# Delta-rule attention and a gated feed-forward on one Trainium2 core: the attention's fp16 pairs and block matrices become fp32 products of one head each

## The chip, the cores and the metric

The kernel runs on one NeuronCore of a Trainium2 chip. The time is device microseconds from one launch; the time before is the median of three runs. The engines that matter are TensorE (PE in the profile, with its weight loads listed as PEld), VectorE (DVE), ScalarE (ACT), GpSimd (POOL) and SyncE (SP), which issues the DMAs.

## The reference

Two parts follow each other. The first is a recurrence over 768 tokens for 4 x 8 = 32 independent heads with 48 features each; the second is a dense product with a gate.

```python
# q, k, v: (4, 8, 768, 48); beta: (4, 8, 768)
k_n = k / (norm(k) + 1e-6)
for t in range(768):
    y[t]   = q[t] @ state                       # state: 48 x 48 per head
    v_old  = state^T k_n[t]
    state += beta[t] * outer(k_n[t], v[t] - v_old)
x = y, heads side by side                       # (3072 tokens, 384)
out = ((x @ w_a) * (x @ w_b)) @ w_out           # w_a, w_b: 384 x 1536, w_out: 1536 x 384
```

## The kernel before

**Chunks.** The recurrence is done in 24 chunks of 32 tokens, in six groups of four (`GROUPS`). The 128 partitions hold four heads' worth of 32 tokens (index `h4`), and eight such fours (index `q`) lie beside each other. The state of all heads lives in PSUM (`S_ps`, 112 partitions by 2 x 384). For every chunk there are: the Gram matrix `ga` of keys with keys and queries (`prep`); a triangular system whose inverse is built row by row on VectorE, with two instructions per row (`solve`, buffers `b`, `tmp`); and in `steps` the products `ks` (keys with state), `up` (inverse with right-hand side), `yp` (queries with state, plus masked attention with `u`) and the update of `S_ps`.

**Precision.** The products of the attention are fp16 with each operand split in a high and a low half, so each product is three matmuls (`THREE`: hi.hi, hi.lo, lo.hi). The halves are made by a ScalarE copy and a subtraction on VectorE, or through TensorE (`VIA_PE`: a matmul by the identity `eye`, a matmul by the negative identity `neg` or `neg1`, a copy out of PSUM). Keys are scaled by 1/norm; queries and values are scaled by a power of two that is found from sums of squares for each group (`total`, `gram`, `qtok` and `vn` loads in `prep`), and `facs` undoes it at the end.

**Block matrices.** `kqbd` (112 x 2 x 16 x 128, four of them) and `tabd` (128 x 2 x 2 x 8 x 128, two of them) hold the heads' small matrices on block diagonals with zeros between them, so that one 112 x 64 or 128 x 128 matmul serves two or four heads. GpSimd and VectorE zero them at the start; VectorE and ScalarE copy the blocks in for every chunk (`kqbd<-kqc`, `tabd<-ta`). The key norms reach the feature-major layout through a DRAM scratch tensor (`rk`, then `rbk`), for group 0 through a matmul.

**Feed-forward.** The weights come as 64-bit floats and are decoded by integer instructions on VectorE in four parts of columns (`weights`, streams `w0`, `w0b`, `w1`, `w2`), then split in halves. `moe` takes two chunks at a time (256 tokens, `xsub`) and walks 12 column blocks `fc`: 18 matmuls of 128 x 128 by 256 (`bank<-x,wsl`), the gate (`a`, `g`, `ghl`), and 6 matmuls by 384 columns (`bank<-wo_hi,ghl`, `bank<-wo_lo,ghl`). There are 12 x 12 = 144 such units.

**Order.** Nothing is issued in program order. `Plan` collects the operations, gives each a modelled duration (`price`) and a priority (`URGENCY` by stream), finds dependencies by the regions that are read and written, and list-schedules all engines in several passes; each engine then gets its instructions in that order. Six PSUM banks are leased to attention, gate and output in turn. Since one helper (line 402) records every instruction, nearly all have the same line in the profile; tiles tell them apart.

**Halved solves.** For groups where `HALVES` is 1 the system of 32 rows is solved as two of 16 in the same instructions (15 rows of steps in place of 31), and the corner is filled with small fp32 matmuls (`bank<-b,ta`, `bank<-b,mk`, `bank<-wr,b`).

## Time and profile before

| | |
|---|---|
| Time, median of three runs (lowest to highest) | 701.37 us (699.37 to 702.09) |
| Span of the profiled execution | 698.7 us |
| PE busy / PEld busy | 644.0 us / 546.2 us |
| DVE busy / ACT busy / POOL busy | 553.3 us / 334.6 us / 27.5 us |
| Mean granted TensorE clock | 0.957 |
| Matmul records | 11454 |
| DMA | 58.36 MB in 32863 packets |

The profiled execution is one of the same program; its span, 698.7 us, lies 2.7 us under the runs' median, and no more of its own time than the span is listed. Busy times are the union of an engine's instructions. A matmul's listed duration includes the time until its result is out (about 0.18 us for the smallest), so that several overlap; what a group costs on the PE is read from its start to the start of the next group in the order of time.

### The profile page before, as it was taken

The page shows a single profiled execution, that of the slowest core. Times are in us where ns is not written, and L with a number is a line of the kernel's source. Part 1 is how long each engine was busy: PE and PEld are TensorE (multiplying, and loading weights), DVE is VectorE, ACT ScalarE, POOL GpSimd, SP SyncE. Part 2 cuts the span into 40 slices and gives each one's busy share as a digit, 9 for nine tenths or more (in the row PEclk, how much of TensorE's full clock was granted, in tenths as well). Part 3 has the DMA queues.
Part 4 walks back from the last instruction along what each step waited for, and adds up shares of the span by engine and source line. Part 5 has one row for each costly group of instructions (what it writes and reads, how often), then busy time and mean ns, then how long its engine had stood idle before and what let it go on. Part 6 is the DMA issues. An engine that isn't in the chain of part 4 may idle for free.

```text
span 698.7 us, 25936 instructions
## 1 busy us (share of the span) xinstructions
PE 644.0 (92%) x11454; PEld 546.2 (78%) x11454; DVE 553.3 (79%) x1385; ACT 334.6 (48%) x786; POOL 27.5 (4%) x50
## 2 busy tenths in 40 slices
PE   2774999899989999999999998999899999999996
PEld 0443668788868888888888887888788888888886
DVE  8999889899657889998899997799797899643221
ACT  2374867655434446455545544445354334342222
POOL 9300000000000000000000000000000000000000
PEclk9976899999968999999999999999999999999999
DMA  9637756314212413243223232132231000100000
GB/s 228 179 111 215 220 151 195 101 35 136 71 60 69 111 40 100 63 106 92 71 69 96 56 100 81 46 92 76 72 88 49 2 22 27 37 26 1 12 13 23
DMA packets 32863, 58.36 MB, mean 84 GB/s; under 512 B 5104, under 2 KB 23280, under 8 KB 32752
## 3 DMA queue, kind: packets, MB, share of 16 engines
q1 hardware_dynamic: 32752, 56.72, 28.6%
q8 instruction: 89, 1.46, 0.9%
q14 instruction: 22, 0.18, 0.1%
HBM read 51.90 MB, written 4.80 MB: 81 GB/s over the span
## 4 chain that ended last, share of the span: by engine, by line
PE 81%; DVE 9%; DMA 5%; issue 3%; ACT 1%; SPq 0%; DVEq 0%; ACTq 0%
PE bank L402 78%; PE S_ps L402 3%; DMA wsl<-in_kqt 2%; DMA raw<-in_kqt 1%; DVE kqc L402 1%; DVE b L402 1%; DVE kqbd L402 1%; DVE wsl L402 1%; DVE tabd L402 1%; DVE x L402 1%; DMA b<-in_wa 1%; DMA t<-in_vn 1%; DVE raw L402 0%; DVE tmp L402 0%; DVE ghl L402 0%
## 5 line engine op out<-in xcount | busy, mean ns | idle before, releaser
L402 PE MATMUL bank<-x,wsl 128*128 128x256 f16 x2592 | 314.0, 275 | 1.7 <-issue 1.1
L402 PEld LDWEIGHTS <-wsl 128*128 128x128 f16 (+1 forms) x2676 | 249.4, 99 | 68.7 <-issue 22.7
L402 PE MATMUL bank<-wo_hi,ghl 128*128 128x384 f32 x576 | 187.4, 364 | 0.3 <-issue 0.2
L402 ACT COPY a<-bank 128x256 f32<-128x256 f32 x144 | 53.6, 372 | 141.3 <-PE bank L402 141.0
L402 PEld LDWEIGHTS bank<-wo_hi,ghl 128*128 128x128 f32 x576 | 107.9, 190 | 3.2 <-issue 0.6
L402 DVE TENSOR_TENSOR g<-bank,a 128x256 f32<-128x256 f32 x144 | 60.7, 421 | 59.8 <-ACT a L402 56.5
L402 PE MATMUL bank<-wo_lo,ghl 128*128 128x384 f32 x288 | 97.9, 340 | 0.0
L402 ACT CAST ghl<-g 128x256 fp32r<-128x256 f32 x144 | 58.1, 404 | 54.7 <-DVE g L402 54.0
L402 PEld LDWEIGHTS <-kqbd 112*64 112x64 f16 x3360 | 60.3, 115 | 17.7 <-issue 13.1
L402 DVE TENSOR_TENSOR ghl<-g,ghl 128x256 fp32r<-128x256 f32 x144 | 60.2, 419 | 14.9 <-ACT ghl L402 14.3
L402 PEld LDWEIGHTS bank<-wo_lo,ghl 128*128 128x128 f32 x288 | 55.2, 192 | 0.3 <-issue 0.2
L402 DVE TENSOR_TENSOR b<-b,tmp 128x31 f32<-128x31 f32 (+20 forms) x154 | 49.3, 320 | 2.1
L402 DVE TENSOR_TENSOR tmp<-b,b 128x31 f32<-128x31 f32 (+20 forms) x154 | 49.0, 318 | 2.1
L402 PE MATMUL bank<-shl,kqbd 112*64 112x48 f16 x2208 | 44.7, 192 | 0.6 <-issue 0.6
L402 DVE COPY tabd<-ta 32x1024 f16<-32x1024 f16 (+1 forms) x96 | 38.6, 402 | 5.4 <-PE bank L402 2.2
L402 PEld LDWEIGHTS <-tabd 128*128 128x128 f16 x1152 | 34.2, 97 | 5.4 <-issue 2.9
L402 ACT ACTIVATE ld<-ld 128x384 f32<-128x384 f32 x60 | 31.2, 522 | 12.9 <-DMA ld<-in_kn 11.0
L402 DVE COPY kqbd<-kqc 48x2048 f16<-48x2048 f16 x48 | 33.6, 701 | 3.1 <-PE bank L402 2.5
L402 PE MATMUL S_ps<-uhl,khl 32*48 32x48 f16 x2208 | 23.5, 186 | 8.8 <-issue 8.7
L402 PEld LDWEIGHTS <-khl 32*48 32x48 f16 x2208 | 20.3, 97 | 13.6 <-issue 12.7
L402 DVE TENSOR_TENSOR shl<-S_ps,shl 112x768 f16<-112x768 f32 x23 | 21.9, 953 | 6.6 <-ACT shl L402 6.5
L402 PE MATMUL bank<-kqc,kqbd 112*64 112x64 f16 x1152 | 23.4, 199 | 2.9 <-DVE kqbd L402 2.4
(138 smaller groups left out, 742.2 us busy)
## 6 DMA issues: line engine op xcount, KB each, us to landing
raw<-in_kqt SPq DMA_DIRECT2D x42, 192.0 KB, 3.7
rbk<-rk SPq DMA_DIRECT2D x40, 128.0 KB, 3.4
stage<-in_wo SPq DMA_DIRECT2D x12, 384.0 KB, 3.8
t<-in_vn SPq DMA_DIRECT2D x24, 192.0 KB, 2.5
t<-in_kn SPq DMA_DIRECT2D x24, 192.0 KB, 3.0
out<-wsl SPq DMA_DIRECT2D x24, 192.0 KB, 2.1
ld<-in_kn SPq DMA_DIRECT2D x20, 192.0 KB, 2.4
ld<-in_qtok SPq DMA_DIRECT2D x20, 192.0 KB, 2.4
```

Source lines behind the costliest of these rows:

```text
L402: fn(*(self.place(a, lease) for a in args), **{k: self.place(a, lease) for k, a in kw.items()})
```

## The change

The attention is computed in fp32 throughout, with one matmul per head and product. The tiles of the array are 64 x 32 (features by tokens, for `ga`, `ks` and the query part of `yp`), 32 x 32 (for `up` and the attention part of `yp`) and 32 x 64 (for `S_ps`): 32 matmuls per product where there were 24, 48 or 96.

- All fp16 halves of the attention, the block matrices `kqbd` and `tabd`, their zeroing, the scratch `rk`, the scaling of keys and queries, and the group scale of q and v go. The key's norm enters the right-hand side instead: `vt` is multiplied by it on GpSimd, and `dc` carries beta over the squared norm.
- Each chunk's keys and values are loaded once (`kns` also serves the squares); `qtok` is no longer loaded. The raw transposed k and q have eight buffers in place of one.
- x is scaled per token by a power of two taken from its norm: a square on ScalarE, six bf16 matmuls by ones (`nt`), five VectorE instructions (`ez`, `fct`, `facs`, and a multiplication of `yT`).
- `HALVES` is kept for group 0 only. The order's priorities (`URGENCY`) change, with group 0 ahead of the weights, and `price` has a formula for small fp32 matmuls.
- `ga` of a group is issued behind the last operation named in `ready` (`dc`, or the end of the previous solve).
- The weights are staged in 3072 columns in place of 2048.

```diff
-HALVES = [1, 1, 0, 0, 0, 0]
+HALVES = [1, 0, 0, 0, 0, 0]
...
+                if ins[0].dtype == F32:
+                    return max(4 * n, 128) / 9.6 + 1.0
...
-    kqbd = [cst.tile([KR, 2, 16, P], F16, name=f"kqbd{i}") for i in range(4)]
-    tabd = [cst.tile([P, 2, 2, 8, P], F16, name=f"tabd{i}") for i in range(2)]
...
+    rawr = ring(cst, "raw", 8, [KR, 2, 16, 32], F32)
+    knr = ring(cst, "kn", 8, [P, 384], F32)
...
+        V.tensor_mul(s1, nm, nm)
+        V.reciprocal(s0, s1)
+        V.tensor_mul(dc, s0, bt[:, g * 32 : g * 32 + 32])
+        ready.append(len(plan.ops) - 1)
...
+            plan.behind = set(ready)
             with plan.group():
-                for q, i, l, rr, pr, _ in pairs():
+                for q, h4, a, _ in heads():
                     T.matmul(
-                        ga[64 * pr : 64 * pr + 64, q, :],
-                        bd[:, l, q * 2 + pr, 0:64],
-                        kqc[:, rr, q * 2 + pr],
+                        ga[tok(h4), q, :],
+                        rw[feat(h4), 0, a],
+                        rw[feat(h4), :, a],
...
+            G.tensor_mul(
+                vt.rearrange("p (q e) -> p q e", e=D),
+                vt.rearrange("p (q e) -> p q e", e=D),
+                nm[:, ci * 8 : ci * 8 + 8].unsqueeze(2).broadcast_to([P, 8, D]),
             )
...
-                A.copy(shl[:, 0], S_ps[0:KR, :, 0:384])
-                V.tensor_sub(shl[:, 1], S_ps[0:KR, :, 0:384], shl[:, 0])
+                sh = shr()
+                A.copy(sh, S_ps[0:KR, :, 0:384])
...
+                            ks[tok(h4), cols],
+                            rw[feat(h4), 0, a],
+                            sh[feat(h4), h4 // 2, cols],
...
+                        up[tok(h4), cols],
+                        tts[c][tok(h4), q],
+                        f32[tok(h4), cols],
...
+            A.activation(sq, yT, AF.Square)
+            nt = att()
+            with plan.group():
+                for j in range(3):
+                    T.matmul(nt[:, 0:P], one16, sqv[:, j], start=(j == 0), stop=(j == 2), skip_group_check=True)
+                for j in range(3):
+                    T.matmul(
+                        nt[:, P : P + 1], sqv[:, j], one16[:, 0:1], start=False, stop=(j == 2), skip_group_check=True
+                    )
...
+            V.scalar_tensor_tensor(yv, zv, 2.0**63, yv, op0=ALU.min, op1=ALU.mult)
```

## The prediction

> **What bounds the kernel now.** I read the page's busy times first, then the chain that ended last, then the stretches, because the shares are an average over very different stages.

> ```profile
> PE 644.0 (92%) x11454; PEld 546.2 (78%) x11454; DVE 553.3 (79%) x1385; ACT 334.6 (48%) x786; POOL 27.5 (4%) x50
> ...
> PE 81%; DVE 9%; DMA 5%; issue 3%; ACT 1%; SPq 0%; DVEq 0%; ACTq 0%
> ```
> ```profile
> 0.00:60.00 60.00, 30.22 (x300) 18.42 (x300) 55.94 (x148) 24.87 (x53) 22.65 (x45) 0.87 0.65 176
> 60.00:100.00 40.00, 35.58 (x982) 23.85 (x983) 34.73 (x91) 30.39 (x74) 0.99 (x1) 0.81 0.68 201
> 100.00:200.00 100.00, 95.75 (x1644) 82.25 (x1645) 83.83 (x208) 60.31 (x143) 0.00 (x0) 0.97 0.36 106
> ```

> The columns of the second fence are PE, PEld, DVE, ACT, POOL, granted clock, DMA share, GB/s. PE is idle for 698.7 - 644.0 = 54.7 us in all, and (60 - 30.22) + (40 - 35.58) = 34.2 us of that falls in the first 100 us. From 100 us on PE is the bound: it is full, and the chain lies on it for 81% of the span. In the first 60 us VectorE is the bound (55.94 of 60). So the change is worth (a) what it takes from or adds to PE in the full stretch and (b) what it does to the start. VectorE or ScalarE work that goes after 100 us is worth nothing by itself.

> **PE: the attention's products.** In the order of time, a group's cost is its start to the next group's start, switch between tile shapes included. One steady chunk:

> ```profile
> 511.21 0.94 PE L402 MATMUL S_ps<-uhl,khl 32*48 32x48 f16 x96
> 512.09 1.16 PE L402 MATMUL bank<-x,wsl 128*128 128x256 f16 x9
> ...
> 516.22 0.94 PE L402 MATMUL bank<-shl,kqbd 112*64 112x48 f16 x48
> 517.09 0.44 PE L402 MATMUL bank<-wo_hi,ghl 128*128 128x384 f32 x1
> ...
> 518.33 0.95 PE L402 MATMUL bank<-kqc,kqbd 112*64 112x64 f16 x48
> 519.22 2.14 PE L402 MATMUL bank<-x,wsl 128*128 128x256 f16 x18
> 521.19 0.77 PE L402 MATMUL bank<-fhl,tabd 128*128 128x48 f16 x24
> 521.80 0.42 PE L402 MATMUL bank<-wo_hi,ghl 128*128 128x384 f32 x1
> ...
> 524.02 0.94 PE L402 MATMUL bank<-shl,kqbd 112*64 112x48 f16 x48
> 524.90 0.78 PE L402 MATMUL bank<-uhl,tabd 128*128 128x48 f16 x24
> 525.61 0.58 PE L402 MATMUL S_ps<-uhl,khl 32*48 32x48 f16 x52
> ```

> `S_ps` 0.88, `ks` 0.87, `ga` 0.89, `up` 0.61, `yp` 0.88 + 0.71: 4.84 us a chunk. A unit of the feed-forward is 1.97 us (18 matmuls of 256 columns, 0.43 ns a column) and 1.24 us (the six after 517.09), 3.2 us; 144 of them are 461 us, about 70% of PE's busy time.

> No row shows a 48-column fp32 product on small tiles. I build it from these:

> ```profile
> 87.45 1.06 PE L402 MATMUL bank<-b,mk 128*128 128x256 f32 x2
> 88.33 0.34 PE L402 MATMUL bank<-uhl,neg 128*128 128x384 f16 x1
> 88.61 0.74 PE L402 MATMUL bank<-b,ta 32*32 32x16 f32 x64
> 89.28 0.42 PE L402 MATMUL bank<-kqc,neg 112*112 112x512 f16 x1
> ...
> 122.10 0.34 PE L402 MATMUL bank<-uhl,neg 128*128 128x384 f16 x1
> 122.27 1.02 PE L402 MATMUL bank<-raw,mk 112*112 112x512 f32 x2
> 123.13 0.38 PE L402 MATMUL bank<-kqc,neg 112*112 112x512 f16 x1
> 123.35 0.39 PE L402 MATMUL bank<-wsl 128*128 128x128 bf16 x4
> 123.67 0.94 PE L402 MATMUL bank<-shl,kqbd 112*64 112x48 f16 x48
> ```

> An fp32 call leaves two records, two passes over its columns. One call of 512 columns took 123.13 - 122.27 = 0.86 us, so a pass costs 0.84 ns a column: 40 ns for 48 columns, 54 ns for the 64 of `ga`. The question is how many of the four tiles run at once. `b,ta` answers it for 32 x 32 tiles. Its moving operand has the same stride as that of `b,mk`, which took 0.88 us for two passes of 256, 1.72 ns a column; so each of its 64 passes takes 27.5 ns, 1.76 us together, and the group took 0.67. At least 2.6 passes ran at once, switch included. Bounds for a group of 32 products with 48 columns (64 passes): four at once and 0.1 us of switch, 64 x 40 / 4 + 100 = 0.74 us; as in `b,ta`, 64 x 40 / 2.6 = 0.98 us. `S_ps` before, four tiles too, needs 0.88 / 24 = 37 ns a turn where 48 fp16 columns stream in 48 x 0.43 = 21 ns, so a turn loses up to 16 ns; I take 46 ns, nearer to four at once since `S_ps` issues a product each 9 ns and an fp32 turn has 40 ns for four: 16 x 46 + 100 = 0.84 us. For `ga` in the same way 0.96 to 1.33, taken 1.06. The six matmuls of `nt`: four of 128 columns took 0.32 with the switch, three of the six have one column; 0.36 taken (0.3 to 0.48). A new chunk is 5 x 0.84 + 1.06 + 0.36 = 5.62 us, 0.78 more than 4.84; times 24, **+19 us** (ends 5.0 and 6.7: +4 to +45).

> [...]

> **PE: what goes.** Making fp16 halves through PE, the group scale, the norm's broadcast, and group 1's halved solve:

> ```profile
> L402 PE MATMUL bank<-raw,mk 112*112 112x512 f32 x10 | 6.2, 705 | 0.0
> L402 PE MATMUL bank<-t,mk 128*128 128x384 f32 x8 | 4.3, 622 | 0.3 <-ACT wsl L402 0.3
> L402 PE MATMUL bank<-uhl,neg 128*128 128x384 f16 x12 | 4.2, 347 | 1.0 <-ACT uhl L402 1.0
> L402 PE MATMUL bank<-ta,neg 128*128 128x256 f16 x12 | 3.8, 351 | 0.1
> L402 PE MATMUL bank<-wsl,mk 112*112 112x512 f32 x6 | 3.0, 604 | 0.0
> ```

> By start to start: 16 records of `raw,mk` and `wsl,mk` (8 calls at 0.86) 6.9; their eight `kqc,neg` at 0.22, 1.8; the norm's four broadcasts, same size, 3.5; `t,mk`, `uhl,neg`, `ta,neg` are 12.3 us busy, about half that by start to start (`uhl,neg` at 122.10: 0.34 listed, 0.17 to the next), 6; the half solve of group 1, four chunks at 0.67 (`b,ta`) + 0.88 (`b,mk`) + about 0.67 (`wr,b`, as many records), 8.9; sums of squares and other small groups an estimated 6. Together **-33 us**, all before about 200 us.

> **The start.** The feed-forward begins in earnest here:

> ```profile
> 99.40 3.11 PE L402 MATMUL bank<-x,wsl 128*128 128x256 f16 x27
> ```

> It needs chunks 0 and 1 and the first two weight parts. VectorE sets this:

> ```profile
> L402 DVE COPY kqbd<-kqc 48x2048 f16<-48x2048 f16 x48 | 33.6, 701 | 3.1 <-PE bank L402 2.5
> L402 DVE SCALAR_TENSOR_TENSOR wsl<-stage,wsl 128x256 int32<-128x256 int32 x12 | 4.9, 416 | 0.0
> L402 DVE TENSOR_TENSOR b<-b,tmp 128x31 f32<-128x31 f32 (+20 forms) x154 | 49.3, 320 | 2.1
> ```
> ```profile
> L402 DVE TENSOR_SCALAR neg<-mk x2: 523/3296/6070, 11.4 to 15.5; 128x128 f16<-128x128 f32 x2
> ```

> What it must do first in the new kernel: two weight parts with 24 two-input decodes at 0.42 (10 us), 12 one-input ones and four `wo` blocks (12, scaled from those by elements); group 0 up to chunk 1, estimated with 0.3 us for an instruction of the solve's kind (`b<-b,tmp`, 320 ns) and 0.4 to 0.6 for the wider ones: norms and sums 5, `gnat` and `ats` 4, half solve 13, two chunks' ends 5, together 27. That makes 49 us. The 16 `kqbd` copies of the first two groups (11 us) and the wait on GpSimd's zeroing (one `neg` instruction took 6.07 us where its twin took 0.52, both of one shape) are gone. At VectorE's 93% of the first 60 us that is 53 us; with waits between engines I take 65 us as the new begin. PE has about 32 us of work before that (four `ga` 4, the half solve of group 0 9, weights 10, two chunks 9). So PE idles about 33 us, as the 34.2 now: **0**. The earlier begin is the same gain as the removed PE work, not a second one. Ends: begin at 55, -10; begin at 85, +20.

> After it, VectorE still owes chunks 2 and 3 (5), two weight parts of twice the width (2 x 24), `prep` (9) and the full solve of group 1 (62 instructions at 0.32, and two transposes: 23; before, 30 shorter ones), about 85 us, and two instructions of 256 columns a unit (0.84). PE in that time has 24 units, 77 us, and 15 us of attention. It fits barely, which is a rival.

> **Parts of no cost, and their cover.** GpSimd's product on `vt`, 24 times: no row of the trace has a product there; the fills, 22.65 us in 45 instructions, are 0.5 us each, and I allow up to four times that, 2 us. Values are loaded up to three chunks ahead, and a chunk has 525.61 - 511.21 = 14.4 us; without that cover each would add its length to a chunk's chain, 48 us at most. It queues with the zeroing of `X` on POOL, five times. The new wait of `ga` for `ready` holds later PE work only if a solve is late. `nt` and its five VectorE instructions (about 1.6 us) stand behind a chunk's end, not in the state's chain; the chain loses the second `S_ps` copy, both halves of `f` and the second of `u`. Fewer DMAs go through SP: `qtok`, `rbk`, `rk` and second loads of k and v go. Eight `raw` buffers allow earlier loads; PE idles 20.5 us in all after 100 us, which bounds what that and every shorter chain can give there. After 100 us VectorE falls by about a third, behind PE: 0.

> **Sum.** 698.7 - 33 + 19 + 0 = 684.7 span; a little less cold clock at the start (0.81 in 60 to 100 us now), -3: 681.7. The profiled span lies 2.7 us under the runs' median: **684 us**, 2.4% faster.

> **Rivals.**
> 1. *The start gets much better:* VectorE's relief lets the feed-forward begin near 55 us, and the tiles reach 0.74 us a group: -10 and -14, 660. For it: VectorE was 93% busy there. Against: the chain through ga, solve, up, S_ps and ks crosses engines.
> 2. [...]
> 3. *Slower: VectorE is late with group 1.* The full solve and the two large weight parts exceed the 24 units' cover by 25 us: 711. VectorE has 105 us of work (85, and 24 units at 0.84) for 92 us of PE work; it decides when VectorE does not keep about 90% busy in that stretch, and it is 84% busy in 100 to 200 us now.
> 4. *No change:* group price 0.98, +40 in place of +19, beside the same -33: 705; or VectorE's relief was hidden anyway and the start is 15 us later.

> **Chances and range.** Main case 0.52, rival 1 0.15, rival 2 0.10, rival 3 0.13, rival 4 0.10. Main case alone: 668 to 697. The range 655 to 716 leaves out rival 2 and the ends of 1 and 3, 0.2 in all. Half a per cent, 3.5 us, is what a measurement of this kernel can tell from no change. Faster by more: 0.67; within: 0.10; slower: 0.23.

> **What would show it.** Right: groups of 64 fp32 records at 0.8 to 0.9 us start to start; `x,wsl` from about 65 us; PE idle 25 to 35 us in the first 100 and full after; VectorE under 65%. Wrong: groups at 1.4 us (rival 2); a hole in PE between 100 and 170 us with solve rows of VectorE in it (rival 3); POOL rows in PE's waits.

## The result: slower, and the profile after

The changed kernel took 732.5 us (median of four runs, 724.5 to 742.5) beside 700.4 us for the kernel before on the same chip: 1.038 times as long, with a 95% interval of 1.033 to 1.043. The ratio is taken from the two lower runs, 724.5 and 727.4 (granted clock 0.97), since the other two, 737.6 and 742.5, ran at 0.94, and of the runs further down one of `rule_early`, of 2849 us, is left out. The profiled execution is the one of 724.5, with a span of 722.6 us. The forecast was 684.

The page of the changed kernel (busy times, then the chain that ended last), and its stretches with the columns PE, PEld, DVE, ACT, POOL, granted clock, DMA share, GB/s:

```profile
PE 639.7 (89%) x13266; PEld 547.5 (76%) x13266; DVE 408.1 (56%) x1133; ACT 238.6 (33%) x545; POOL 26.8 (4%) x34
...
PE 81%; DVE 7%; issue 6%; DMA 5%; SPq 1%; ACT 1%; ACTq 0%
```
```profile
0.00:60.00 60.00, 29.48 (x716) 22.66 (x720) 42.09 (x131) 14.27 (x31) 2.92 (x8) 1.00 0.86 235
60.00:100.00 40.00, 34.68 (x1293) 27.72 (x1286) 19.38 (x53) 17.40 (x39) 2.15 (x2) 0.91 0.37 110
100.00:200.00 100.00, 83.33 (x1802) 70.41 (x1803) 85.21 (x230) 41.25 (x89) 7.23 (x7) 0.91 0.25 73
200.00:400.00 200.00, 188.52 (x3872) 162.88 (x3875) 113.52 (x319) 64.81 (x151) 7.73 (x9) 0.99 0.14 40
400.00:600.00 200.00, 188.98 (x3921) 163.22 (x3910) 110.17 (x308) 64.48 (x149) 6.78 (x8) 0.99 0.08 23
```

VectorE fell below the forecast 65%, from 79% to 56%. PE has 4.3 us less to do by its busy time, but it idles 82.9 us instead of 54.7. Of that, 35.8 us lie in the first 100 us (34.2 before, 33 forecast). The growth comes behind: 16.7 us in 100 to 200, where it was 4.3, 22.5 us in 200 to 600, where it was 10.7, and 7.9 after that (5.6 before). In 200 to 600 us VectorE is busy for only 56%. In the chain, "issue" has doubled from 3% to 6%. "Issue" is time in which an engine waits for nothing that the profile shows. PE's own waits from 200 to 616 us that the profile puts down to "issue" (us in total, times and longest), first of the kernel before, then of the changed one. The changed kernel has no others there; the kernel before has 3.2 us more behind VectorE and ScalarE:

```profile
PE S_ps L402 <- issue: 5.1, 3, 2.5
PE bank L402 <- issue: 2.3, 4, 1.1
```
```profile
PE bank L400 <- issue: 13.2, 17, 2.2
PE S_ps L400 <- issue: 10.2, 7, 2.1
```

In the order of time, such holes stand inside groups of small products, where no operand can be missing, since the rest of the group has the same ones. The changed kernel:

```profile
415.49 1.10 PE L400 MATMUL bank<-raw 48*32 48x64 f32 x64
416.40 0.85 PE L400 MATMUL bank<-sh,raw 48*32 48x48 f32 x60
418.39 0.28 PE L400 MATMUL bank<-sh,raw 48*32 48x48 f32 x4 [1.14 <-issue]
418.59 0.88 PE L400 MATMUL bank<-u,at 32*32 32x48 f32 x64
419.41 0.92 PE L400 MATMUL S_ps<-u,kn 32*48 32x48 f32 x60
422.41 0.40 PE L400 MATMUL S_ps<-u,kn 32*48 32x48 f32 x4 [2.08 <-issue]
```

Between the two holes lie 4 + 64 + 60 = 128 matmul records. Counting PE's matmul records from the first on, I found every hole of 0.35 us or more of the changed kernel after 200 us at the same place in a row of 128 (the number of the record ahead of the hole, modulo 128, is 81 to 87, drifting slowly over the program; some records are missing from a trace). A matmul and its weight load are two instructions (the page lists 13,266 of each), so 128 records are 256 instructions. The DMA queue that the page names "instruction" gives the size of it, before and after:

```profile
q8 instruction: 89, 1.46, 0.9%
```
```profile
q8 instruction: 103, 1.69, 1.0%
```

These are packets, MB and share: 16,384 bytes a packet, one for each 128 records (103 x 128 = 13,184 of 13,266). In the trace of the changed kernel the packet of a block starts 2.2 to 2.9 us before such a hole ends, and the next packet 1.1 to 2.3 us after it. In quiet stretches it starts some 145 records ahead of the block's first record, which is just before PE enters the block ahead of it. So in these traces PE's program arrives in blocks of 128 matmuls, the fetch of the next one starts within some 2 us of the begin of the one before, and PE stands still where it works off 128 records faster than a block arrives. Small fp32 products do that: two groups of 64 records need 1.63 us, and from the end of one hole above to the end of the next, 418.39 to 422.41, it took 4.02.

**A balance.** I compared each record's start-to-start time with the usual one of its form and sorted the excess by place: at a block's edge, other holes of 0.35 us or more, and the rest, which stays with the work. Worked out from the traces, in us:

| | PE's work | block edges | other waits | ahead of the first and behind the last matmul | span |
|---|---|---|---|---|---|
| before | 626.4 | 17.4 | 43.8 | 11.1 | 698.7 |
| changed | 624.0 | 47.7 | 34.4 | 16.5 | 722.6 |
| changed, `fetch_aware` (below) | 612.9 | 15.6 | 28.1 | 14.2 | 670.8 |

The block edges alone (+30.3) are more than the whole loss (+23.9).

### The profile page after: what moved, and what is told of

Read it like the earlier page. It is cut to its first block, busy times and chain, and to the rows that moved or that the text cites. A ratio compares the mean times of both kernels' runs of the same rounds, so it can differ in the third digit from the quotient of the medians.

```text
span 722.6 us, 28838 instructions
## 1 busy us (share of the span) xinstructions
PE 639.7 (89%) x13266; PEld 547.5 (76%) x13266; DVE 408.1 (56%) x1133; ACT 238.6 (33%) x545; POOL 26.8 (4%) x34
## 4 chain that ended last, share of the span: by engine, by line
PE 81%; DVE 7%; issue 6%; DMA 5%; SPq 1%; ACT 1%; ACTq 0%
PE bank L400 77%; PE S_ps L400 3%; DMA raw<-in_kqt 3%; DVE wsl L400 2%; DVE b L400 1%; DVE x L400 1%; DMA stage<-in_wo 1%; DMA v<-in_vn 1%; SPq L400 1%; DVE tmp L400 1%; DVE ghl L400 0%; DVE g L400 0%; DVE ss L400 0%; DMA out<-wsl 0%; ACT y L400 0%
## 5 line engine op out<-in xcount | busy, mean ns | idle before, releaser
L400 ACT CAST ghl<-g 128x256 fp32r<-128x256 f32 x144 | 58.3, 405 | 70.0 <-DVE g L400 63.5
L400 PE MATMUL bank<-sh,raw 48*32 48x48 f32 x2944 | 43.8, 207 | 4.9 <-issue 3.1
L400 PEld LDWEIGHTS bank<-sh,raw 48*32 48x32 f32 x2944 | 36.5, 109 | 14.2 <-issue 9.5
L400 DVE STREAM_TRANSPOSE yt<-y 128x384 f32<-128x384 f32 x24 | 13.9, 578 | 54.3 <-ACT y L400 54.3
L400 PE MATMUL bank<-raw 48*32 48x64 f32 x1536 | 33.0, 243 | 7.0 <-DMA raw<-in_kqt 3.5
L400 PEld LDWEIGHTS bank<-raw 48*32 48x32 f32 x1536 | 28.1, 123 | 13.2 <-issue 5.1
L400 PE MATMUL S_ps<-u,kn 32*48 32x48 f32 x1472 | 25.4, 211 | 14.1 <-issue 14.1
L400 PEld LDWEIGHTS S_ps<-u,kn 32*48 32x48 f32 x1472 | 21.0, 124 | 16.4 <-issue 14.0
L400 POOL TENSOR_TENSOR v<-v,nm 128x384 f32<-128x384 f32 x24 | 21.6, 904 | 318.4 <-DMA v<-in_vn 221.9
L400 PE MATMUL bank<-u,at 32*32 32x48 f32 x1536 | 24.2, 207 | 7.6 <-issue 7.6
L400 PEld LDWEIGHTS bank<-u,at 32*32 32x32 f32 x1536 | 19.7, 108 | 10.4 <-issue 8.8
```

What stands on the lines that cost most here:

```text
L400: fn(*(self.place(a, lease) for a in args), **{k: self.place(a, lease) for k, a in kw.items()})
```

## Experiments

There are two theories. FETCH is what is described above. The rival, ARRAY: the holes come from the tiles of the array or from changing between shapes. Beside them stand VECTORE (VectorE is late with group 1) and ORDER (the new priorities let too much fall into one stretch), for the hole at 100 to 200 us, where PE waited for VectorE:

```profile
109.75 0.40 PE L400 MATMUL bank<-wsl 128*128 128x128 bf16 x4 [1.03 <-DVE wsl L400]
111.40 1.69 PE L400 MATMUL bank<-raw 48*32 48x64 f32 x64 [1.25 <-DVE g L400]
113.02 0.61 PE L400 MATMUL bank<-wsl 128*128 128x128 bf16 x4
...
123.98 0.84 PE L400 MATMUL bank<-wo_hi,ghl 128*128 128x384 f32 x2
...
125.68 0.51 PE L400 MATMUL bank<-wo_hi,ghl 128*128 128x384 f32 x2
...
130.40 0.63 PE L400 MATMUL bank<-wo_hi,ghl 128*128 128x384 f32 x2 [2.46 <-DVE ghl L400]
```

### The stream alone (`bench`)

```diff
+    for section in SECTIONS:
+        for _ in range(section[0]):
+            small(section[1], section[2])
+            if section[3]:
+                large(section[3])
...
+SECTIONS = [(24, 48, 32, 0), (24, 16, 32, 0), (24, 48, 32, 16), (24, 48, 32, 4), (12, 192, 32, 0), (24, 96, 16, 0)]
```

The four numbers of a section are its groups, the columns and the fp32 products of 32x32 weights in each, and the large matmuls (fp16, 128x128 by 256) behind each.

> Leaves out the whole computation; its output is a constant. It measures streams of fp32 products of 32x32 weights on constant data, in six sections parted by 128 large matmuls (fp16, 256 columns): (1) 24 groups of 32 products with 48 columns, back to back, 1536 records; (2) the same with 16 columns; (3) each group of (1) followed by 16 large matmuls; (4) followed by 4; (5) 12 groups with 192 columns; (6) 24 groups of 16 products with 96 columns. Theory FETCH (PE's program arrives in blocks of 128 matmuls with their weight loads, and a block takes about 3.8 us when the next is asked for late): (1) 12 blocks, 45 us; (2) also 45 us although it has a third of the columns; (3) 61 to 65 us, nearly without holes; (4) 13 blocks, 48 us; (5) 31 us, set by the array; (6) 23 us, six blocks. Theory ARRAY (the holes come from the tiles or from the change of shape): (1) 24 x 0.815 = 20 us; (2) 13 us at most; (3) 61 us; (4) 30 us; (5) 31 us; (6) 16 to 20 us.

The six sections as stretches (length; PE, PEld, DVE, POOL, granted clock, DMA share, GB/s), and the beginnings of the first and the second:

```profile
16.49:58.50 42.01, 20.39 (x1533) 18.67 (x1535) 0.00 (x0) 0.00 (x0) 0.92 0.02 4
74.36:115.80 41.44, 21.09 (x1531) 19.80 (x1533) 0.00 (x0) 0.00 (x0) 0.56 0.02 4
131.98:193.97 61.99, 61.99 (x1894) 51.87 (x1896) 0.00 (x0) 0.00 (x0) 1.00 0.01 4
209.93:256.50 46.57, 34.42 (x1622) 25.95 (x1624) 0.00 (x0) 0.00 (x0) 1.00 0.02 4
272.69:303.80 31.11, 31.11 (x766) 23.69 (x768) 0.00 (x0) 0.00 (x0) 1.00 0.01 3
318.12:338.10 19.98, 16.95 (x769) 15.76 (x767) 0.56 (x1) 0.00 (x0) 1.00 0.02 4
```
```profile
16.62 2.58 PE L67 MATMUL small<-u,k 32*32 32x48 f32 x223
21.23 2.78 PE L67 MATMUL small<-u,k 32*32 32x48 f32 x128 [2.04 <-issue]
24.68 1.56 PE L67 MATMUL small<-u,k 32*32 32x48 f32 x128 [0.68 <-issue]
...
78.45 1.48 PE L67 MATMUL small<-u,k 32*32 32x16 f32 x128 [1.92 <-issue]
81.90 1.90 PE L67 MATMUL small<-u,k 32*32 32x16 f32 x128 [1.97 <-issue]
```

48 columns or 16, the stream takes 42.0 and 41.4 us, and there is a hole every 128 records. With 16 large matmuls behind each group there is no hole (PE busy 61.99 of 61.99), with 4 there is (34.42 of 46.57), and 192 columns fill the time too. The sixth section, 19.98 us, lies under FETCH's 23 and within ARRAY's 16 to 20, so its length speaks for neither; but its four holes of 0.35 us or more also stand 128 records apart, at the same place in a row of 128 as those of sections 1, 2 and 4. FETCH holds, ARRAY falls. From hole to hole a block took 3.45 to 4.0 us where the next was wanted at once, 3.7 on average over the ten blocks behind the first hole of each of the first two sections: close to the 3.8 expected. The sections came out shorter than 45 us because their first 223 records ran through without a hole. The DMA engines are nearly idle here (share 0.02), and yet a block's packet starts 2.3 to 2.9 us before such a hole ends, as in the kernel; so the wait needs no other transfers in the way.

### Undoing one part (`halves1`, `urgency_before`)

```diff
-HALVES = [1, 0, 0, 0, 0, 0]
+HALVES = [1, 1, 0, 0, 0, 0]
```

> One part of the change undone: group 1 is solved in halves on PE again (HALVES[1] = 1). Theory VECTORE (VectorE is late with group 1 between 100 and 170 us and that costs 12 us or more): the hole of PE in 100 to 200 us shrinks from 16.7 us to under 8 and the time falls by 8 to 15 us, to about 710 to 717 against 724.5. Theory FETCH alone (the hole is secondary, the half solve puts 4 x 130 more small records on PE): 720 to 728, no change that can be measured.

```diff
-URGENCY = {"first": 5000, "prep0": 5000, "solve0": 5000, ...}
+URGENCY = {'w0': 100, 'w0b': 800, 'w1': 300, ...}
```

> One part of the change undone: the table of urgencies is the one of the kernel before, all else is the changed kernel. Theory ORDER (the new table lets the weight parts of 512 columns and the solve of group 1 fall into one stretch): the feed-forward begins within 5 us of 95, VectorE is more evenly busy from 60 to 170 us, and the time is 8 to 15 us shorter, 710 to 717. Theory FETCH: the table moves work about but the bursts of attention stay, 722 to 735.

734.8 us (1.051, 1.046 to 1.057) and 739.1 us (1.056, 1.049 to 1.063): no gain, so both theories of a gain missed, and both times lie above FETCH's ranges as well. The granted clock was 0.94 and 0.93 in the profiled executions, against 0.976 in that of the changed kernel, so whether the two are really slower than it stays open. In the first, the other waits in 100 to 200 us fell from 12.6 to 5.2 us, in the second to 0.2, but block edges rose from 47.7 in all to 54.8 and 52.8. In the second, the first matmul also came at 21.4 us in place of 10.8, which costs more than the edges. The hole at VectorE can be removed and nothing is won in these two orders; that the late blocks alone ate the gain isn't shown.

### The planner told of the blocks (`fetch_aware`)

The instructions stay those of the changed kernel; only their order differs. `pairs` holds an operation's matmul records; `seen` counts them, `due` is when the next block can be there, and `BLOCK` is 3800 ns.

```diff
+            if seen >= self.FIRST and (seen - self.FIRST) % 128 == 0:
+                lost += max(0.0, due - t)
+                t = max(t, due)
+                due = t + self.BLOCK
...
+                rank = lambda k: (self.fetched(ops[k], t, ops[k].dur, seen, due)[0] > self.FETCH) * 1e9
+                can[e] = [(pri[k] + rank(k), k) for _, k in can[e]]
```

> The changed kernel with the same instructions; only the planner differs: it counts PE's matmul records in blocks of 128, lets a block begin no sooner than 3.8 us after the one before it, and where a group of small products would meet a block that is not there yet it takes another group that is ready. Theory FETCH: the holes put down to issue in 200 to 616 us fall from about 30 us to under 12, and the time falls by 15 to 30 us, to 695 to 710. Theory ARRAY: the holes stay where the small groups are (they number the same), there are more changes of shape, and the time is 724 or more.

672.6 us, 0.962 of the kernel before (0.958 to 0.967): the fastest of the kernels here that compute everything, and a larger gain than even FETCH expected (695 to 710). Its stretches, and all of PE's waits from 200 to 616 us:

```profile
0.00:60.00 60.00, 30.33 (x652) 23.23 (x656) 47.30 (x143) 17.43 (x38) 3.29 (x8) 0.77 0.89 244
60.00:100.00 40.00, 30.45 (x1196) 25.08 (x1184) 30.39 (x70) 19.34 (x39) 1.94 (x2) 0.74 0.61 185
100.00:200.00 100.00, 97.41 (x2208) 84.74 (x2207) 77.86 (x218) 43.84 (x98) 5.90 (x8) 1.00 0.15 43
200.00:400.00 200.00, 197.86 (x4568) 170.91 (x4566) 120.94 (x337) 70.83 (x163) 9.31 (x11) 0.98 0.16 45
400.00:600.00 200.00, 199.96 (x4161) 173.96 (x4159) 115.83 (x325) 69.62 (x162) 5.10 (x6) 1.00 0.05 17
```
```profile
PE bank L429 <- issue: 1.8, 1, 1.8
PE bank L429 <- ACT sq L429: 0.3, 1, 0.3
```

PE is now full from 100 us on, with the same 13,266 records. By the balance, 32.1 of the 51.8 us of span that it gained over the changed kernel are block edges; 6.3 are other waits, 2.3 lie at the ends, and 11.1 are PE's work itself, which I can't split further: the granted clock rose from 0.91 to 1.00 in 100 to 200 us but fell in the first 100 (0.77 and 0.74 in place of 1.00 and 0.91), and holes too short to be counted are in it too.

### Where the gain lies (`rule_late`, `rule_early`)

```diff
-            if e == "PE" and not back and self.FETCH and len(can[e]) > 1:
+            if e == "PE" and not back and self.FETCH and 3000 <= seen < 1000000 and len(can[e]) > 1:   # rule_late
+            if e == "PE" and not back and self.FETCH and 0 <= seen < 3000 and len(can[e]) > 1:         # rule_early
```

Only the choice of the next group is limited: the planner's own times count the blocks from the first record on in both, so an order can change also where the rule is off.

> The changed kernel, the rule only for records from number 3000 on (from about 175 us). FETCH: the holes of 200 to 616 us go, about 25 us of the 52 us that the whole rule gave: 695 to 705; the hole at 100 to 200 us stays. If the gain came from the start alone: 720 to 730.

> The changed kernel, the rule only for records up to number 3000 (until about 175 us). If the hole at 100 to 170 us, where PE waited for VectorE, is a late effect of PE's fetch in the first 100 us, it shrinks to under 6 us and the time falls by 10 to 25 us, to 700 to 715, with the holes of 200 to 616 us left. If the hole is VectorE's own (rival 3 of the forecast): 722 to 730.

`rule_late`: 700.1 us (1.002, 0.999 to 1.006). The block edges after 200 us fell from 30.2 to 2.3 us, and the ratio from 1.038 to 1.002, some 25 us, as FETCH expected. The two do not match one to one, since the start changed too: the feed-forward began at 112.2 us in place of 94.9. `rule_early`: 718.6 us (1.027, 1.022 to 1.033), some 7 us less, between its two expectations. Its 100 to 200 us, then those of `rule_late`:

```profile
100.00:200.00 100.00, 90.14 (x2203) 77.08 (x2191) 73.26 (x206) 41.79 (x92) 7.01 (x8) 0.95 0.18 48
```
```profile
100.00:200.00 100.00, 81.33 (x1705) 68.50 (x1704) 84.36 (x236) 43.63 (x94) 7.41 (x7) 0.91 0.25 73
```

With the early rule the waits other than block edges in this stretch are 2.0 us (12.6 in the changed kernel). So the hole at VectorE is no matter of how much VectorE has to do: the same instructions in another order close it. That it followed from fetch alone isn't shown, since the whole order of the start differs. The two halves of the rule give 25 and 7 us alone, some 52 together; the stretch from about 175 to 200 us, where the early rule has ended and edges return (9.9 us in 100 to 200), is part of the difference. The feed-forward began at 100.3 us in `rule_early`, at 112.2 in `rule_late` and at 89.8 in `fetch_aware`; that may be much of the rest, which stays open.

### The block's price in the rule (`block3500`)

```diff
-    BLOCK = 3800.0
+    BLOCK = 3500.0
```

> The changed kernel with the rule for the whole program and 3.5 us for a block, which is what the stream of small products alone measured (41.99 and 41.42 us for 12 blocks), in place of 3.8. FETCH: a rule a little too mild leaves a few more holes, 668 to 680. If the gain of 3.8 was one lucky order: 685 or more.

673.5 us (0.964, 0.958 to 0.969): the gain does not hang on the one order that 3.8 us gave.

### The kernel before, with the rule (`before_fetch_aware`, `before_rule_late`)

The same edit on the kernel before; in the second, the condition `1800 <= seen` is added.

> The kernel before, its instructions unchanged, with the planner's rule for PE's blocks of 128 records. If the rule is worth what the kernel's own holes are worth (FETCH: some 10 us put down to issue in 200 to 616 us, 5 more in 100 to 200): 680 to 690. Then the changed kernel with the same planner (672.6) is the faster by 8 to 17 us, and the forecast's price for the products was right and only the fetch was missing. If the rule is just a luckier order: anything from 690 to 710, and the changed kernel's gain can't be put down to fetch.

> The kernel before with the rule only for records from number 1800 on (from about 122 us), so that its start stays. Under the rule for the whole program its feed-forward began at 115 us in place of 99, which may have eaten the gain. FETCH: the begin stays within 4 us of 99, the 15 us of block-edge holes after 100 us fall by half or more, and the time is 685 to 695. If the rule does nothing for this kernel: 697 to 705.

703.2 (1.009, 1.005 to 1.012) and 703.7 us (1.007, 1.004 to 1.010). Both expectations of a gain missed. Block edges fell only from 17.4 to 13.6 and 13.5 us, and the feed-forward began later, at 115 and 111 us in place of 99, also where the rule was off in the start. So these runs don't tell what the rule would bring with the old start kept. By the expectation as it was written, a result in 690 to 710 says that the changed kernel's gain can't be put down to fetch on the strength of the rule alone. What puts it there in part is the balance above (32.1 of 51.8 us) and `rule_late`; the remainder of the gain may be the order's. Among the orders tried the kernel before stays at 700 us, while the changed one reaches 672.6.

### The begin of the feed-forward (`loads_behind`, `warm`, `full0`, `lo_on_vector`, `no_w12`, `no_w`)

`loads_behind` (no rule):

```diff
+            plan.behind = {loaded[2]} if g == 1 else set()   # before the loads of kn, and again before those of raw
```

> The changed kernel, planner without the rule; only the loads of k and q of group 1 (kn and raw, 2.4 MB) stand behind the loads of the third weight part on SP's queue, in place of ahead of the second. If these early loads hold up the weights (LOADS: 0.86 of the DMA engines are busy in the first 60 us at 235 GB/s, and 2.4 MB at that rate are 10 us): the second weight part is ready up to 10 us sooner, the feed-forward begins at 85 to 90 us in place of 95 to 99, and the time falls by 5 to 10 us. If PE's fetch and VectorE set the begin anyway: 720 to 730, the begin within 3 us of 95.

732.7 us (1.052, 1.045 to 1.058). The DMA share of the first 60 us fell from 0.86 to 0.71, the begin came at 99 us, and nothing was won. LOADS falls in this form, as far as one order can tell.

`warm`, `full0` and `lo_on_vector` stand on `fetch_aware` (the last with 3.5 us a block):

```diff
+            if g == 0 and k >= 6:                # warm: for nine steps of group 0's solve
...
+                with plan.group():
+                    T.matmul(S_ps[:, 0, 384:400], one16, tick, start=True, stop=True, skip_group_check=True)
+                    for _ in range(14):
+                        T.matmul(S_ps[:, 0, 384:512], one16, one16, start=True, stop=True, skip_group_check=True)
-HALVES = [1, 0, 0, 0, 0, 0]                      # full0
+HALVES = [0, 0, 0, 0, 0, 0]
-LO_W = 'PPVV'                                    # lo_on_vector
+LO_W = 'PVVV'
```

> The changed kernel with the rule, and nine bundles of 15 idle matmuls (128x128, bf16, on constants, results unused) that PE works off while VectorE solves group 0, from about 35 to 48 us. [...] If the chain in the start crosses engines and loads anyway: 670 to 680, with the begin unchanged.

> The changed kernel with the rule, group 0 solved in full on VectorE too (HALVES[0] = 0): PE loses 4 x 130 small records in the start, about four blocks, VectorE gets 32 more instructions of 0.3 us before the first state. If PE's fetch and clock set the begin (FETCH): four blocks at 3.8 us go, VectorE adds 10 us, 664 to 674. If VectorE's solve sets the begin: it comes about 10 us later and the time is 678 to 688.

> The changed kernel with the rule at 3.5 us a block (673.5), the low halves of the second weight part made by VectorE (6 instructions of 256 columns, about 0.4 us each) in place of PE (6 x 2 fp32 passes of 256 columns at 0.43 each when cold, 6 matmuls with the unit matrix, 6 copies). PE WORK: 6 to 8 us of PE go before the begin, which comes 4 to 8 us earlier, 664 to 670. If PE's work is not what holds the begin: 670 to 678.

679.0 (0.972), 677.1 (0.970) and 678.5 us (0.973): each 4 to 7 us slower than without, and the begin at 95.6, 97.3 and 92.4 us (89.8 in `fetch_aware`, 92.5 with 3.5 us a block). No gain came in any; `full0` lies between its two expectations and `lo_on_vector` just above its second. In `warm` the groups ran faster, 0.82 us from start to start where the changed kernel had 1.3, but `fetch_aware` has them at that pace from about 60 us on already, so there was little left to win. The changed kernel, then `warm`:

```profile
61.10 1.50 PE L400 MATMUL bank<-u,at 32*32 32x48 f32 x64
62.39 0.76 PE L400 MATMUL bank<-b,kk 32*32 32x16 f32 x41
```
```profile
59.37 0.88 PE L429 MATMUL bank<-v,tt 32*32 32x48 f32 x64
60.19 0.28 PE L429 MATMUL bank<-wsl,neg 128*128 128x256 f16 x1
```

So neither a faster pace of PE, nor the half solve or the second part's low halves taken from it, brought the begin forward. In `full0` VectorE got the half solve's work and the begin came 7.5 us later, so VectorE's solve may weigh there; `warm` moved it by 5.8 us without such a reason, so a new order alone can do nearly as much. `no_w12` and `no_w` leave weights out, the first the two later parts, the second all four, and are read for the begin alone:

```diff
-    run_all(ws[2])   # and ws[3]; in no_w also ws[0] and ws[1], and a constant stands for all weights
+                whalf[m, j, fc] = whalf[m, j, fc % 4]
```

> The changed kernel with the rule (3.8 us a block), the weight parts of 512 columns left out: neither loaded nor decoded, the feed-forward uses the first two parts again in their place. Read for the begin of the feed-forward (89.8 us with them), not for the time. If their loads and decoding hold the begin (LATER PARTS: the chain of waits in the first 105 us lay on loads of weights for 41%): begin at 70 to 80. If not: 87 to 97.

> The same with all weights left out, constants in their place, so that nothing but the attention of group 0 stands before the feed-forward. If the attention's own chain holds the begin (ATTENTION: ga, solve, half solve, then four chunks one after another across engines): 80 or later. If the first two weight parts hold it, by PE's work on them (10 us at full clock) and VectorE's decoding: 60 to 70.

The first feed-forward matmuls of the changed kernel, of `fetch_aware`, `no_w12` and `no_w`:

```profile
94.89 2.14 PE L400 MATMUL bank<-x,wsl 128*128 128x256 f16 x9
```
```profile
89.80 2.12 PE L429 MATMUL bank<-x,wsl 128*128 128x256 f16 x9
```
```profile
80.19 0.37 PE L429 MATMUL bank<-x,wsl 128*128 128x256 f16 x1 [0.17 <-ACT x L429]
```
```profile
63.54 2.10 PE L429 MATMUL bank<-x,wcon 128*128 128x256 f16 x9
```

The attention alone reaches the begin at 63.5 us. The expectation had 60 to 70 if the weights hold the begin. The first two weight parts add 17 us (80.2 in `no_w12`, at the edge of its expected 70 to 80), and the later two, which nothing needs yet, add 10 more. Each of these kernels was run once, and since other orders moved the begin by 3 to 8 us, the 10 are a rough number.

## Why the prediction was wrong, point by point

- **The products' price: right, and a little high.** From 200 us on, groups of 64 fp32 records took 0.815 us (`ks`, `up`, the query part of `yp`), 0.81 (its other part) and 0.87 (`S_ps`) where no block edge fell into them, against 0.84; `ga` 0.92 to 1.03 against 1.06, `nt` 0.25 to 0.31 against 0.36. A chunk is 5.40 us at most against 5.62, which makes +13 of the +19. Rival 2, in which the passes of a group follow one another and a group takes 1.4 us, is out for 64-row tiles as well: the quiet stretches show nothing near that. Groups of 1.3 to 1.9 us do occur in the first 200 us of the changed kernel (`ga` 1.62 at 111.40), but the large matmuls beside them are slow too: a pair of `wo_hi,ghl` is listed with 0.84 us at 123.98 and 0.51 at 125.68.
- **PE's work: the total came out, its parts did not.** -33 and +19 make -14, and by the balance `fetch_aware` has 13.5 us less work than the kernel before. With +13 for the products, what went would be 27 and not 33, so two errors of some 6 us cancel; that is luck. No run measures the 33 by itself, and the changed kernel as it stands has only 2.4 us less.
- **The step that set the sign: a term put at nothing.** The prediction took PE's time as a sum of array times and changes of shape, called PE full from 100 us on, and passed over "issue" at 3% of the chain. It was there in the trace of before (17.4 us of block edges). The change takes a chunk from 288 records in its small groups to 390 (384 in the products, six in `nt`), a group's records follow each other at 12.7 ns (0.815 us for 64), and the order runs the attention in bursts of four chunks. One block of such records then lasts less than half of the 3.45 us or more that the next one takes to come. This term is +30.3 us, and it makes the sign. The claim that a shorter chain can only help, "PE idles 20.5 us in all after 100 us, which bounds what that and every shorter chain can give there", failed with it: a denser burst idles more.
- **The start: here "That makes 49 us" of VectorE work and the 65 us from it failed.** I counted what VectorE must do first, took it as busy for 93% of the time, and took the rest as going behind. The begin came at 94.9 us, outside the range of 55 to 85, and VectorE was busy for 42.1 of the first 60 us, which is 70%; it was no longer the bound. In the chain of waits up to 105 us PE's own `bank` rows have 38% and the loads of `raw` 21%. The idle time of PE came out right all the same (35.8 us against 33), but by luck: the forecast had 32 us of work and then the begin at 65, while PE worked 64 of the first 100 us in a start that lasted 30 us longer. 65 us is close to what the attention takes alone (63.5); the weights stand in its way with 26 us in `fetch_aware`, the later parts among them, though I had put those after the begin. Rival 1, a begin near 55 us, is out with it.
- **Rival 3 came in part.** PE waited for VectorE at 110 to 131 us, as it said. But its cause, too much work for VectorE (whose price has a slip: 684 and 25 make 709, not 711), is not what the runs show: `rule_early` and `fetch_aware` have the same work and 2.0 and 0.6 us of such waits. Undoing the full solve (`halves1`) did not make the kernel faster.
- **VectorE's relief:** its busy time after 100 us fell by a quarter (463 to 347 us), not by a third.
- **Parts of no cost: held, as far as seen.** GpSimd's product on `vt` is 0.90 us each, within the allowed 2, and no wait of PE names it. The early loads of group 1 that eight `raw` buffers allow went ahead of the second weight part on SP's queue; putting them behind gave nothing.
- **What would have told it:** of the signs named, the groups' price, the idle time in the first 100 us (nearly: 35.8 against 25 to 35) and VectorE's share came as forecast. The begin of `x,wsl` and "full after" did not, and the row behind the latter is the one that the prediction should have looked for in the trace of before: holes inside a group of equal products.

## What to carry to other kernels

When a change makes more and shorter matmuls, count instructions as well as array time: in these runs 128 matmuls with their weight loads had to last some 3.5 to 4 us, else PE waited for its program. A hole put down to "issue" in the middle of a group of equal instructions was the sign here (2.08 us at 422.41 in the changed kernel). The cure that worked here was not fewer instructions but an order that puts large matmuls between the small groups: it took 52 us off the changed kernel, 32 of them at block edges, and turned a loss of 4% into a gain of 4%. On the kernel before, with fewer edges to save and a later start, the same rule gained nothing. And a stage's begin that several engines prepare is not forecast by the work of the busiest one: leave parts out, and see which of them moves it.
